# Five score groups in each column by Strassen's seven products, summed two at a time, with all score slots in one tile

## The chip, the cores and the metric

The kernel runs on one core of one Trainium2 chip. The metric is the device time of one execution in microseconds (us); a kernel's time is the median over its runs. A profile is one execution recorded by the hardware profiler. In it PE is TensorE's matmul, PEld its weight load, DVE is VectorE, ACT is ScalarE, POOL is GpSimd and SP is SyncE; L482 is line 482 of the kernel file.

## The reference

A gated attention without softmax is followed by a feed-forward layer with a gate of its own:

```python
batch, seq, d_model = (8, 3008, 256); d_qk = 64
scale = 1.0 / S
scores = scale * np.matmul(z, z.transpose(0, 2, 1))
attn = np.maximum(scores, 0.0) ** 2
out = np.matmul(attn, v)
x = (u * out).astype(np.float32)          # reshaped to 24064 tokens of 256
...
h = x @ w_in                              # 256 -> 2048
g = h * np.cos(h)
return (g @ w_out).astype(np.float32)     # 2048 -> 256
```

All inputs and the output are float32 in device memory; the kernel works on them as 16-bit floats and accumulates in 32 bits. Since the scores are z times its own transpose, the score matrix of a batch is symmetric.

## The kernel before

**Units.** A batch of 3008 tokens is cut into 6 *columns* of 512 queries (the last has 448). Keys are cut into 24 blocks of 128 (the last has 64), four blocks make a *group* R of 512 keys. So a batch has 6 x 6 squares (column c, group R) of 512 by 512 scores. Time is planned by hand in units, 8 to a column, 48 to a batch: `at(t, rank, f)` notes an event, the events are sorted by time and rank, and run in that order. TensorE's matmuls are chained, so they stay in this order; the other engines' instructions are put in order by the scheduler of the language, within their data dependencies and the ordering edges that `after(...)` adds. The edge from `before[-1]` keeps an instruction behind the last matmul emitted so far.

**Scores.** `s_visit` handles three half squares at once: `s_matmuls` (L271) writes six score banks with 64-row matmuls (the two 64-row halves of the array run side by side), then `s_squares` lets ScalarE do the relu (L307) and VectorE the square (L309), into one of 18 slots in SBUF. There are 14 visits in a batch. Only squares with R >= c are computed; the mirrored one comes from a transpose by DMA on SP's queue (`turn_s`, L321). A diagonal square (R = c) is computed as a triangle, four strips of 512, 384, 256 and 128 columns (L288, L293), and its missing parts are filled by three small transposes (L296). Scores run ahead of their use by `lead`, 1.75 columns.

**Attention times v.** For each column the products with v add up in two accumulator banks. The plain path (`av_bank`, L362) takes two matmuls of 512 columns for each block of keys, eight for a group. The other path is Strassen's scheme in Winograd's form: a group is treated as a 2 x 2 matrix of halves (2 x 128 keys by 256 queries) times a 2 x 2 matrix of halves of v (2 x 128 keys by 128 features); `product(b, c, n)` for n = 1 to 7 (L482) does one of the seven products for all groups of the set `WSET[c]`, two matmuls of 256 columns for each group. It needs sums of score halves, made on VectorE in place in the slots: `a_sums1` makes two sums (L439, L441), the second one into an extra slot, and `a_sums2` (L451) makes two more in one operation after products 2 and 5 have read the old contents. `v_sums` makes four sums of v for each group (L409, L411, L412). `keep` (L496 to L507) copies and adds the parts that several results share. `PLAN` says in which unit of the column each product runs (P1 to P7) and where the blocks left over go (A and B, the two accumulators); `SUM1`, `SUM2`, `WADD`, `RADD` and `TSUM` place the sums. `WSET` has groups 0 to 2 in columns 0 to 3, and 0 to 3 in columns 4 and 5. Columns 0 to 3 of the first batch use no such products; of these, columns 0 to 2 are computed directly, without symmetry. The last 64 keys are a 64-row pair of matmuls (`av_half`, L339), and `finish` (L389) multiplies by u.

**Feed-forward.** 47 tiles of 512 tokens. `h_quantum` does 128 of the 2048 hidden features: two matmuls of 512 columns (L516), a sine on ScalarE (L520), a multiply on VectorE (L523). `y_quantum` does four output matmuls of 256 columns (L533) on the tile before; the sixteenth is followed by a copy on ScalarE and a store (L540). Hidden and output quanta are spread evenly through the units.

**Buffers.** PSUM has six work banks (`ps_w`), shared by scores, hidden tiles and output tiles, and two accumulator banks. v lives in a ring of four tiles of eight blocks, three to a batch; all loads (L121) go through POOL's queue, and `hold` keeps a load behind the last matmul emitted so far. Transposes of u, z and scores are issued on SP.

Of the kernel before, what the change touches and what calls it, by code (L numbers as in the profile page):

```python
# [14 lines left out]
def kernel(  # L15
# [33 lines left out]
    NW = 4  # L49
    PLAN = {  # L50
        0: [(1.0, 'P1 P2'), (1.4, 'P5'), (2.35, 'P6 B1'), (2.55, 'B1'), (3.0, 'P7 B1'),
            (3.4, 'P3'), (4.55, 'A1'), (4.75, 'A1'), (5.4, 'P4 B2'), (6.15, 'A1 B2'),
            (6.35, 'A1 B1'), (6.55, 'A2'), (6.75, 'A1'), (7.0, 'A1 B2'), (7.4, 'A3 B1')],
        1: [(1.0, 'P1 P5 P2'), (2.35, 'P6'), (3.0, 'P7 B1'), (3.4, 'P3'), (4.15, 'B1'),
            (4.35, 'A1 B2'), (4.55, 'A1'), (4.75, 'P4 B1'), (5.4, 'B2'), (6.35, 'A1 B1'),
            (6.55, 'A2 B2'), (6.75, 'A5'), (7.0, 'A1'), (7.4, 'B1')],
        2: [(0.75, 'P1 P5 P2'), (1.4, 'P6'), (2.15, 'B1'), (2.75, 'B1'),
            (3.0, 'P7 P3 B1'), (4.55, 'B1'), (4.75, 'B1'), (5.0, 'P4 B1'),
            (5.4, 'A2 B1'), (6.15, 'A1'), (6.35, 'A2'), (6.55, 'A1 B1'), (6.75, 'B1'),
            (7.0, 'A1 B1'), (7.4, 'A4 B1')],  # L60
        3: [(1.0, 'P1 P5 P2'), (2.15, 'P6 B1'), (2.75, 'B3'), (3.0, 'P7'), (3.4, 'P3'),
            (4.55, 'A1 B1'), (5.0, 'A1'), (5.4, 'A1 B2'), (6.15, 'P4 A1'),
            (6.35, 'A1 B1'), (6.55, 'A1 B1'), (6.75, 'A1'), (7.0, 'A2 B1'),
            (7.4, 'A2 B1')],
        4: [(0.75, 'P1 P5'), (1.0, 'P2'), (2.15, 'P6'), (3.0, 'P7'), (3.4, 'P3 A1'),
            (4.35, 'B1'), (4.55, 'P4'), (4.75, 'A1 B1'), (5.0, 'B1'), (5.4, 'B1'),
            (6.15, 'A1 B1'), (6.55, 'A1'), (6.75, 'A1 B1'), (7.0, 'B1'), (7.4, 'A2')],
        5: [(1.0, 'P1 P5'), (1.4, 'P2'), (2.15, 'P6'), (2.55, 'B1'), (3.0, 'P3'),
            (3.4, 'P7 B2'), (4.75, 'A1'), (5.0, 'P4'), (5.4, 'A1 B1'), (6.15, 'A1 B1'),
            (6.35, 'A2'), (6.75, 'A1'), (7.0, 'B2'), (7.4, 'A1')],  # L70
# [181 lines left out]
    def slot(*key):  # L252
        return slots[slot_of[key]].rearrange("p (s k w) -> p s k w", s=K, w=P)

    def seven(b, c):

        return [] if (b, c) <= (0, NC // 2) else WSET[c]

    def s_matmuls(b, c, R, p):


        zt = zT[b % 2]
# [496 lines left out]
```

## Time and profile before

| what | value |
|---|---|
| median of 10 runs | 1214.7 us (1213.78 to 1217.81) |
| the profiled execution | 1214.06 us, its span 1211.9 us |
| granted TensorE clock | 1.00 |
| hidden matmuls L516 / output matmuls L533 | 1504 x 379 ns / 3008 x 273 ns |
| plain products with v L362 / Strassen products L482 | 1024 / 2072 matmuls |
| multiplies L523, squares L309 on VectorE | 752 x 688 ns, 254 x 689 ns |
| sines L520, relus L307 on ScalarE | 752 x 621 ns, 489 x 616 ns |
| from one batch to the next | 150.6 us (column 4's first products start at 385.25 and 535.87) |

How to read it: a mean duration of a matmul contains the time to run through the array, so matmuls that follow each other overlap; what one costs in a stream is the distance from start to start. The same holds, less strongly, for the vector and scalar engines. The chain that ended last is followed back from the last instruction, at each step to what released it. Between two batches of the steady middle part nothing changes but the data, so one batch can stand for six.

### The profile page before, as it was taken

Reading aid. Unit: us, or ns where it says so; the run is one execution under the profiler, and the core shown is the slowest. Engines: PE = TensorE matmul, PEld = TensorE weight load, DVE = VectorE, ACT = ScalarE, POOL = GpSimd, SP = SyncE. Lnnn points to the kernel's source line nnn. Section 1 sums busy time; section 2 is a strip of 40 time slices with the busy share of each in tenths; the row PEclk is TensorE's granted clock in tenths of the full one; section 3 lists DMA queues with packets and bytes.
Section 4 is the critical chain, followed back from the end, with each engine's and each line's share of the span. In section 5 each row is a group of like instructions: output and inputs, shape, how many; then the busy total and the mean of one; then the engine's idle time right before and its main releaser. Section 6 shows DMA issues by size and latency. Waiting matters only on the chain.

```text
span 1211.9 us, 22944 instructions
## 1 busy us (share of the span) xinstructions
PE 1204.7 (99%) x8421; PEld 766.3 (63%) x8421; DVE 1020.5 (84%) x1995; ACT 831.7 (69%) x1741; POOL 146.1 (12%) x201
## 2 busy tenths in 40 slices
PE   8999999999999999999999999999999999999998
PEld 3356666666666666666666666666666666666666
DVE  7888888888888888888888888888888888888875
ACT  6767767677776776767777677676776767767555
POOL 3210101001010010101101101011110111100000
PEclk9999999999999999999999999999999999999999
DMA  9997968679586795957968569596695857956411
GB/s 153 199 161 120 150 98 129 106 120 154 103 119 109 118 155 103 132 103 111 155 103 134 100 112 163 94 133 104 110 162 94 133 105 113 158 94 120 73 33 48
DMA packets 484225, 145.02 MB, mean 120 GB/s; under 512 B 432400, under 2 KB 484112, under 8 KB 484112
## 3 DMA queue, kind: packets, MB, share of 16 engines
q1 hardware_dynamic: 356448, 88.73, 44.4%
q0 software_dynamic: 100400, 29.77, 25.1%
q10 hardware_dynamic: 27264, 25.06, 6.4%
q8 instruction: 66, 1.08, 0.4%
q14 instruction: 47, 0.39, 0.1%
HBM read 60.29 MB, written 24.64 MB: 70 GB/s over the span
## 4 chain that ended last, share of the span: by engine, by line
PE 99%; ACT 1%; DVE 0%; issue 0%; ACTq 0%; DVEq 0%
PE w L533 27%; PE w L516 27%; PE acc L482 19%; PE acc L362 18%; PE w L271 6%; PE acc L339 1%; ACT rt L307 0%; PE w L716 0%; DVE s L309 0%; ACT zT L227 0%; PE w L222 0%; DVE rt L305 0%; DVE x L389 0%; ACT c L520 0%; ACT ob L540 0%
## 5 line engine op out<-in xcount | busy, mean ns | idle before, releaser
L520 ACT ACTIVATE c<-w 128x512 f16<-128x512 f32 x752 | 437.4, 621 | 258.8 <-PE w L516 215.2
L523 DVE TENSOR_TENSOR g<-w,c 128x512 f16<-128x512 f32 x752 | 494.1, 688 | 61.2 <-ACT c L520 59.6
L533 PE MATMUL w<-w_out,g 128*128 128x256 f16 x3008 | 448.6, 273 | 0.0
L516 PE MATMUL w<-x,w_in 128*128 128x512 f16 x1504 | 445.7, 379 | 0.0
L533 PEld LDWEIGHTS <-g 128*128 128x128 f16 x3008 | 294.3, 98 | 191.2 <-issue 0.4
L362 PE MATMUL acc<-s,v 128*128 128x512 f16 (+1 forms) x1024 | 290.6, 378 | 0.4 <-DVE s L309 0.3
L307 ACT ACTIVATE rt<-w 128x512 f16<-128x512 f32 x489 | 253.3, 616 | 44.1 <-PE w L271 44.1
L309 DVE TENSOR_TENSOR s<-rt 128x1024 f16<-128x1024 f16 x254 | 173.0, 689 | 86.0 <-ACT rt L307 84.8
L516 PEld LDWEIGHTS <-w_in 128*128 128x128 f16 x1504 | 147.0, 98 | 73.3 <-issue 3.5
L482 PE MATMUL acc<-s,vsum 128*128 128x256 f16 (+1 forms) x1184 | 154.7, 270 | 0.0
L121 POOL DMA_DIRECT2D ust<-in_u_dram x112 | 81.3, 732 | 556.4 <-PE acc L362 534.8
L362 PEld LDWEIGHTS <-v 128*128 128x128 f16 x1024 | 95.2, 98 | 78.4 <-issue 29.9
L482 PEld LDWEIGHTS <-vsum 128*128 128x128 f16 x1184 | 114.9, 98 | 18.1 <-issue 3.0
L482 PE MATMUL acc<-s,v 128*128 128x256 f16 (+1 forms) x888 | 115.2, 270 | 0.0
L451 DVE TENSOR_TENSOR s<-s,s 128x1024 f16<-128x1024 f16 (+1 forms) x148 | 93.1, 673 | 3.5 <-PE acc L482 3.5
L482 PEld LDWEIGHTS <-v 128*128 128x128 f16 x888 | 83.7, 98 | 19.2 <-issue 11.5
L271 PE MATMUL w<-zT 64*128 64x512 f16 (+3 forms) x684 | 90.4, 359 | 2.4 <-ACT zT L227 1.6
L540 ACT ACTIVATE ob<-w 128x256 f32<-128x256 f32 x188 | 71.3, 379 | 8.4 <-PE w L533 8.4
L288 ACT ACTIVATE rt<-w 128x512 f16<-128x512 f32 (+3 forms) x176 | 62.9, 452 | 11.8 <-PE w L271 11.8
L121 POOL DMA_DIRECT2D v<-in_v_dram x40 | 31.4, 793 | 299.1 <-PE acc L482 146.5
L389 DVE TENSOR_TENSOR x<-acc,ut 128x512 f16<-128x512 f32 (+7 forms) x112 | 64.4, 600 | 2.2 <-PE acc L362 2.1
L441 DVE TENSOR_TENSOR s<-s 128x512 f16<-128x512 f16 (+1 forms) x148 | 60.6, 415 | 1.9
(37 smaller groups left out, 361.3 us busy)
## 6 DMA issues: line engine op xcount, KB each, us to landing
out_dram<-ob ACTq DMA_DIRECT2D x92, 256.0 KB, 2.4
ust<-in_u_dram POOLq DMA_DIRECT2D x80, 128.0 KB, 4.2
v<-in_v_dram POOLq DMA_DIRECT2D x16, 512.0 KB, 6.4
s<-s SPq DMA_TRANSPOSE x249, 4.4
v<-in_v_dram POOLq DMA_DIRECT2D x8, 448.0 KB, 9.5
zst<-in_z_dram POOLq DMA_DIRECT2D x14, 128.0 KB, 4.6
ust<-in_u_dram POOLq DMA_DIRECT2D x16, 96.0 KB, 4.9
w_in<-in_moe_w_in_dram POOLq DMA_DIRECT2D x4, 256.0 KB, 6.4
```

Source lines behind the costliest of these rows:

```text
L121: hold(nc.gpsimd.dma_start(dst, src))
L271: chain(nc.tensor.matmul(sp[:, s0 * P:], zt[h, R * K + k + 1 - lo, :], zt[h, j0 + s0:j0 + K, :].rearrange("p j w -> p (j w)"), start=True, ...
L307: nc.scalar.activation(rt[:, i, :], banks[k], AF.Relu)
L309: ins = nc.vector.tensor_tensor(t.rearrange("p s k w -> p k s w")[:, 2 * p:2 * p + 2], rv, rv, ALU.mult).ins
L362: chain(nc.tensor.matmul(acc[:, 0:wn], vs(b, j // G)[:, j % G, nh * P:(nh + 1) * P], a, start=(start and n == 0), stop=(last and n == len( ...
L451: after(nc.vector.tensor_tensor(dst, src, sub, ALU.subtract).ins, before[-1], NOSYNC)
L482: chain(nc.tensor.matmul(acc[bank][:, cols], lhs[:, k, :], rhs[:, k, :] if old else rhs[:, :, k * P:(k + 1) * P], start=(n in (1, 5) and i ...
L516: chain(nc.tensor.matmul(hp, w_in16[:, k, ft * P:(ft + 1) * P], x[:, k, :], start=(k == 0), stop=(k == NDH - 1)))
L520: nc.scalar.activation(c16, hp, AF.Sin, bias=math.pi / 2.0, scale=inv_s2)
L523: nc.vector.tensor_tensor(gs[(m, ft // FG)][:, ft % FG, :], hp, c16, ALU.mult)
L533: chain(nc.tensor.matmul(ys[m][:, 0:D], gs[(m, f4)][:, ft % FG, ts * P:(ts + 1) * P], w_out16[:, ft, :], start=(ft == 0), stop=(ft == NFT ...
L540: nc.scalar.activation(obs[m][:, i, :], ys[m][:, 0:D], AF.Copy, bias=0.0, scale=inv_s2)
```

## The change

`WSET` gets groups 0 to 4 in every column: 30 groups in a batch in place of 20. All score slots become one tile, so that one access pattern can reach two slots: `teams` pairs neighbouring groups that are stored the same way, and `a_sums1` does its two sums for a pair at once, unless the slots are more than 15 apart. `v_sums` does two groups at once, in four operations; the ordering edge is on the first of them. The second sum has a tile of its own. Diagonal squares become one item of a visit (`t_matmuls`), with their two shorter strips in banks that two diagonals may share. In each visit the third half square is squared on ScalarE (`on_act`). Visits are packed anew, run 2.0 columns ahead, and are shifted singly (`VSHIFT`). The plan tables are all new; the three v loads of a batch move (`VAT`; third before second); hidden tiles come four in a row, followed by sixteen output matmuls (`HOFF`, `YOFF`).

```diff
-    NW = 4
+    NW = 5
     PLAN = {
...
+        3: [(0.75, 'P1 P2'), (1.0, 'P5'), (2.15, 'P6'), (2.35, 'B1'), (2.75, 'P7 P3'),
+            (3.4, 'B1'), (4.75, 'A1'), (5.0, 'A1'), (5.4, 'B1'), (6.15, 'P4'),
+            (6.75, 'A1')],
...
+        5: [(0.75, 'P1 P2'), (1.4, 'P5'), (2.35, 'P6'), (3.0, 'P3'), (4.55, 'P7 B1'),
+            (5.0, 'P4'), (5.4, 'B1'), (6.15, 'A1'), (6.55, 'A1'), (6.75, 'A1'),
+            (7.4, 'B1')],
     }
...
-    TSUM = [-2.9, -0.9, -0.8, 3.5, 3.5]
-    XEND = 4.0
-    WSET = {0: [0, 1, 2], 1: [0, 1, 2], 2: [0, 1, 2], 3: [0, 1, 2], 4: [0, 1, 2, 3], 5: [0, 1, 2, 3]}
+    TSUM = [-1.4, 0.5, 0.1]
+    WSET = {0: [0, 1, 2, 3, 4], 1: [0, 1, 2, 3, 4], 2: [0, 1, 2, 3, 4], 3: [0, 1, 2, 3, 4], 4: [0, 1, 2, 3, 4], 5: [0, 1, 2, 3, 4]}
+    VAT = [-13, -3.9, -4.5]
+    HOFF, YOFF = [0.3, 0.4, 0.4, 0.6], [0.6, 0.7, 0.7, 0.7]
...
-    slots = [kpool.tile([P, K * CW], FP16, name=f"s{i}") for i in range(NSLOT)]
-    vsum = [kpool.tile([P, 4, 2, P], FP16, name=f"vsum{R}") for R in range(NW)]
+    slots = kpool.tile([P, NSLOT, K * CW], FP16, name="s")
+    second = kpool.tile([P, NW, 2, CW // 2], FP16, name="s2")
+    vsum = kpool.tile([P, NW, 4, 2, P], FP16, name="vsum")
...
+    def t_matmuls(b, c, banks, mixed, i):
+        score(b, c, c, 0, 0, 0, banks[0])
+        score(b, c, c, 1, 1, 1, banks[1][:, 0:3 * P])
+        score(b, c, c, 2, 1, 2, mixed[0][:, i * 2 * P:(i + 1) * 2 * P])
+        score(b, c, c, 3, 0, 3, mixed[1][:, i * P:(i + 1) * P])
...
+        if on_act:
+            nc.scalar.activation(sq, rv, AF.Square)
+        else:
+            ins = nc.vector.tensor_tensor(sq, rv, rv, ALU.mult).ins
...
+                s_squares(*pair, banks, on_act=i in (2,) and not direct(*pair[:3]))
...
+    def v_sums(b, g):
+        n = min(2, NW - 2 * g)
+        t = vs(b, g)[:, 0:n * K, :].rearrange("p (r k) (d w) -> p r k d w", r=n, w=P)
+        o = vsum[:, 2 * g:2 * g + n]
+        for d in range(2):
+            ins = nc.vector.tensor_tensor(
+                o[:, :, 2 * d], t[:, :, 2 * d:2 * d + 2, 1], t[:, :, 0:2, d], ALU.subtract).ins
+            if d == 0:
+                after(ins, before[-1], NOSYNC)
+        nc.vector.tensor_tensor(o[:, :, 1], t[:, :, 2:4, 1], o[:, :, 0], ALU.subtract)
+        nc.vector.tensor_tensor(o[:, :, 3], t[:, :, 2:4, 0], o[:, :, 1], ALU.subtract)
...
+    def quarters(b, c, team, first, *step):
+        i, ks, ts = where(b, c, team[0])
+        at = lambda kk, tk: kk * ks + tk * ts
         dims = [(at(*step[0]), 2)] if step else []
+        if len(team) == 2:
+            dims.append(((where(b, c, team[1])[0] - i) * K * CW, 2))
+        return bass.AP(slots.tensor, slots.offset + i * K * CW + at(*first),
+                       (slots.ap[0], *dims, (CW, 2), (1, wide(b, c) // 2)))
...
+    def teams(b, c):
+        out = []
+        for R in seven(b, c):
+            if out and len(out[-1]) == 1 and by_key(b, c, R) == by_key(b, c, out[-1][0]):
+                out[-1].append(R)
+            else:
+                out.append([R])
+        return out
+
+    def a_sums1(b, c, team):
+        if len(team) == 2 and abs(where(b, c, team[0])[0] - where(b, c, team[1])[0]) > 15:
+            for R in team:
+                a_sums1(b, c, [R])
+            return
+        s1 = quarters(b, c, team, (0, 1))
+        after(nc.vector.tensor_tensor(s1, s1, quarters(b, c, team, (1, 1)), ALU.add).ins,
               before[-1], NOSYNC)
         nc.vector.tensor_tensor(
+            s2(b, c, team[0], len(team)), s1, quarters(b, c, team, (0, 0)), ALU.subtract)
...
-    lead = 1.75 * U
-    NV = 3
+    lead = 2.0 * U
+    VSHIFT = {4: -0.27, 13: 0.82, 1: 0.27, 5: 0.0, 2: 0.27, 12: 1.09, 10: 0.27, 7: 0.0, 0: 0.27, 6: 0.29, 9: -0.55, 3: -0.28, 11: 0.54, 8: 0.0}
...
-            at(th + ft // 4 * 2 + ft % 4 * 0.2, 1, lambda m=m, ft=ft: h_quantum(m, ft))
+            at(th + ft // 4 * 2 + HOFF[ft % 4], 1, lambda m=m, ft=ft: h_quantum(m, ft))
...
-                at(th + U + 2 * ts + 0.1 + 0.2 * f4, 4,
+                at(th + U + 2 * ts + YOFF[f4], 4,
...
-                at(t + (-1.5, -0.4, -0.1)[g] * U, 0, lambda b=b, g=g: load_v(b, g))
+                at(t + VAT[g], 0, lambda b=b, g=g: load_v(b, g))
```

## The prediction

> **What bounds the kernel now.** I read the page's busy table and its chain of waits first, then the stretches of equal length, then the chain in order of time, then the groups with shapes kept apart, and last the DMA issues and one score visit in the timeline.
>
> ```profile
> PE 1204.7 (99%) x8421; PEld 766.3 (63%) x8421; DVE 1020.5 (84%) x1995; ACT 831.7 (69%) x1741; POOL 146.1 (12%) x201
> ...
> PE 99%; ACT 1%; DVE 0%; issue 0%; ACTq 0%; DVEq 0%
> ```
>
> TensorE is busy for 99% of the span and makes 99% of the chain that ends last. Busy shares of PE can flatter, so the stretches matter more (time, then busy time of PE, PEld, DVE, ACT, POOL, granted clock, DMA share):
>
> ```profile
> 0.00:50.00 50.00, 46.48 (x245) 16.82 (x246) 41.11 (x72) 32.74 (x61) 14.46 (x24) 1.00 1.25 167
> 300.00:450.00 150.00, 150.00 (x1067) 97.29 (x1065) 128.01 (x254) 105.10 (x222) 17.27 (x25) 1.00 0.79 120
> ...
> 1180.00:1212.00 32.00, 28.78 (x213) 20.45 (x211) 18.02 (x27) 17.42 (x35) 0.00 (x0) 1.00 0.15 51
> ```
>
> From the second batch on PE has no gap, at a granted clock of 1.00; the 7 us that it misses lie in the first 75 us and at the very end. VectorE has 22 us spare in 150, ScalarE 45. So time goes down exactly as matmul columns go away, as long as nothing else becomes late. What a matmul costs in a stream is its pitch in the chain in order of time (start, length, count):
>
> ```profile
> 59.82 2.59 PE acc L362 x12
> ...
> 385.25 2.62 PE acc L482 x24
> 410.06 1.53 PE acc L482 x16
> ```
>
> A 512-column product of the plain path takes 2.59/12 = 215.8 ns, a 256-column Strassen product 2.62/24 = 109.2 ns, a 224-column one (last column of a batch) 1.53/16 = 95.6 ns.
>
> **The change, part by part.**
>
> *Products.* A group (512 keys by 512 queries) costs 8 plain matmuls or 14 half-wide ones. Columns 0 to 3 go from 3 to 5 groups, 4 and 5 from 4 to 5; batch 0 uses the scheme in columns 4 and 5 alone. That is 7 x 8 + 7 + 7 + 2 = 72 more groups, 8 of them in the last, 448-wide column. Building the kernel confirms it: 1024 plain matmuls become 448, 2072 products become 3080. A wide group saves 8 x 215.8 - 14 x 109.2 = 197.6 ns. A 448-column plain matmul has a mean 26 ns under the 512 one:
>
> ```profile
> L362 PE MATMUL acc<-s,v 128*128 128x512 f16 x960 | 273.2, 380 | 0.4 <-DVE s L309 0.3
> L362 PE MATMUL acc<-s,v 128*128 128x448 f16 x64 | 20.0, 354 | 0.0
> L451 DVE TENSOR_TENSOR s<-s,s 128x1024 f16<-128x1024 f16 x116 | 74.1, 688 | 2.7 <-PE acc L482 2.7
> L439 DVE TENSOR_TENSOR s<-s 128x512 f16<-128x512 f16 x116 | 47.8, 419 | 0.0
> L309 DVE TENSOR_TENSOR s<-rt 128x1024 f16<-128x1024 f16 x254 | 173.0, 689 | 86.0 <-ACT rt L307 84.8
> L227 ACT COPY zT<-w 128x1024 f16<-128x1024 f16 x2 | 2.0, 1016 | 2.6 <-PE w L222 2.6
> ```
>
> so 190 ns, and a narrow group saves 8 x 190 - 14 x 95.6 = 182 ns. The sum is 64 x 0.1976 + 8 x 0.182 = **14.1 us less on PE**. Score matmuls stay at 684, feed-forward matmuls at 4512, visits at 14 a batch, each 64-row pair still stands right behind a visit, and SP gets 3 transposes more than its 249; so nothing else moves in amount.
>
> A rule speaks against this step. The Trainium skill (TensorE: Matmul & The Clock Gate, Back-to-back issue gap) says that in a stream of weight loads and matmuls both set the spacing, with about 81 ns at 128 columns and 131 ns at 512. A straight line gives an estimate of 98 ns at 256; eight plain matmuls would be 1048 ns, fourteen products 1372, and the change would add 23 us and end near 1238. The rows above (215.8 and 109.2, proportional to columns, with a weight load before each) contradict it, so I use the rows.
>
> *Vector work*, from the rows above and their 448-wide, 256-wide and v-sum neighbours, by means. Second sums: 148 become 220, 180 x 0.688 + 40 x 0.620 = 148.6 against 93.1, +55.5. First sums: 296 small ones become 88 small and 176 of double size, 72 x 0.421 + 16 x 0.385 + 144 x 0.688 + 32 x 0.620 = 155.4 against 120.6, +34.8. Sums of v: 36.0 against 30.0. One diagonal group more: +1.3. Against that 59 squares go to ScalarE or vanish: -59 x 0.689 = -40.7. Together +57 us: VectorE at 1077 of some 1198, 90%; its spare time in a batch goes from 22 to about 13 us. The cover is that PE waits for none of this directly, only through buffers; ScalarE gets 57 squares at the nearest row, 1.016 us (58 us), and loses 4: 886 us, 74%. I cost both at nothing. A run of four multiplies takes 2.48 us, so one operation more in a queue is worth (2.48 - 0.69)/3 = 0.60; late once in each batch it would cost 7 x 0.6 = 4.2 us (kept as upper bound; a gain is excluded, PE has no wait to lose).
>
> One more price is on a page only. The Trainium skill (ScalarE: Activation LUTs, What ACT_TABLE_LOAD costs) gives about 2.66 us for a switch between table sets. If the new Square were in another set than the sine, 57 x 2 switches would be an estimate of 303 us. The trace shows a single table load, of 1283 ns, and the changed kernel's instruction list also has a single one, so my sum holds nothing for it.
>
> *Waits for banks.* The feed-forward work is regrouped: four hidden tiles in a row, then 16 output matmuls, where before they alternated. A score visit needs all six work banks, so the vector work queued since the last visit must be through. Now the total of PE's waits at visits is 0.5 us. Counting pitches in the changed order, the last hidden tile lies 2.1 to 5.1 us ahead of each visit (1.2 to 2.5 before), and between two visits vector work is at most 0.8 us more than PE's, where 5.1 us of distance follow. I take zero.
>
> *The fifth group of column 3.* Its scores come only just in time. Before product 5 needs the sum, PE has the visit 0.75, the 64-row pair 0.22, 3 plain matmuls 0.65, hidden 1.73, outputs 1.74, products 1 and 2 2.18, eight matmuls of product 5 0.87: 8.1 us. Against it stand, at the same place before the change:
>
> ```profile
> 656.17 0.82 PE L271 MATMUL w<-zT 64*128 64x512 f16 x6
> 656.60 3.05 ACT L307 ACTIVATE rt<-w 128x512 f16<-128x512 f32 x6 [0.53 <-PE w L271]
> 657.71 0.69 DVE L309 TENSOR_TENSOR s<-rt 128x1024 f16<-128x1024 f16 x1 [1.20 <-ACT rt L307]
> ...
> 658.47 4.93 SPq L321 DMA_TRANSPOSE s<-s  x2
> ```
>
> 2.3 us to the issue of the transpose on SP, 4.3 to 5.6 us to its landing (the DMA issues of this place in three batches), 0.42 for the sum: 7.0 to 8.3. That is 0 to 0.2 us, seven times; I take 0.5 us in all. The transpose view has landings of 7.9 us under load; those would cost 2.6 us a batch. While VectorE waits, the hidden-tile multiplies queue behind it, then PE's hidden tiles.
>
> *Loads of v.* The third v load now goes out ahead of the second (on POOL's queue its three DMAs, the second's one, then those of u), behind product 3 of column 5, which frees the ring buffer. Part of its sum carries no ordering edge any more, and in the built order it stands on VectorE right behind two diagonal squares of the visit in that column. PE has 5.7 us between product 3 and that visit (6 hidden 1.30, product 7 0.96, one plain, 2 hidden 0.43, outputs 1.74, product 4 0.96, switch 0.1), then 1.06 to the first square, 0.65 for two: the load has 7.4 us.
>
> ```profile
> v<-in_v_dram POOLq DMA_DIRECT2D x16, 512.0 KB, 6.4
> ...
> v<-in_v_dram POOLq DMA_DIRECT2D x8, 448.0 KB, 9.5
> ```
>
> The last is this very load, at a place where the DMA share was 1.41 (730 to 740 us); the other two v loads, at quieter places, take 6.4. Everything behind the wait shifts: the squares, four multiplies, the column's end, then the sums of v for groups 2 and 3, which product 5 of the next column reads. From the visit to that reading PE has 11.7 us (visit 0.65, pair 0.22, five plain 1.08, 8 and 8 hidden 3.46, 32 outputs 3.48, products 1 and 2 2.18, four matmuls 0.44, switches 0.2), VectorE 3.6 until the visit's work is through, 2.4 for four multiplies, 4.9 for twelve items: 10.9. The second sums right behind, which product 3 reads, are tighter by my count, 0.5 us, and that I take as the slack. I take a landing midway, 8.0 us: 0.6 late, 0.1 after slack, 7 batches, **0.7 us**. Ends: 0, and with the slowest landing seen, 11.4, 3.5 x 7 = 24.5 us.
>
> *The head.* Three such sums (0.42 + 0.42 + 0.29 = 1.1 us) also move into batch 0's first column, where VectorE runs nearly back to back, and score visits start 2 units earlier. Idle gaps of 0.61 and 0.18 us there absorb most: 0.7 us taken, 0 to 2.
>
> *Sum.* -14.1 + 0 + 0.5 + 0.7 + 0.7 = -12.2 us. The profiled execution took 1214.06 (span 1211.9 and 2.1 around it): 1201.9. It lay 0.6 under the median of ten, 1214.7, so I predict **1202.5 us**.
>
> **The rivals.** *The wait for v eats the gain (slower).* One mechanism: the third v load lands after VectorE reaches its sum. At 9.5 us it costs 7 x 1.6 = 11.2, giving 1213; from 14.1 - 1.2 = 12.9, that is a landing of 9.7 us, the change loses; at 11.4 it ends at 1214.7 - 14.1 + 1.2 + 24.5 = 1226. For it: the median of this load. Against it: the place is new, two plain transposes and the next v load share the engines there, not the diagonal's.
>
> *Part of the gain goes into buffers and transposes:* 0.6 to 1.2 us a batch, 4 to 9 us, 1206 to 1211. For it: spare vector time shrinks by 40%. Against it: hidden tiles stand further from the visits.
>
> *VectorE becomes the bound.* If each of 98 visits in seven batches waited for one 0.60 us operation, +59 us, 1260. Against it: 136 us of vector work in 148.6 us of a batch.
>
> *The single tile orders too much.* If sums of two slots waited for every slot between, 88 team sums losing 1 us twice would add about 176 us. Against it: in the built order these sums wait for transposes of their own, and no wait on other readers appears.
>
> **How the numbers follow.** Forecast (1199.5 to 1206) 0.70; part of the gain 0.14; v wait (1211 to 1226) 0.10, 0.03 of it within the bound below; VectorE 0.04; single tile 0.02. A change of 0.2%, 2.4 us, is about what this kernel's measurement can tell from none. Faster: 0.70 + 0.13 = 0.83; within: 0.01 + 0.03 = 0.04; slower: 0.07 + 0.04 + 0.02 = 0.13. The range runs from no wait at all less a pitch error of 1 us, 1199.5, into the second case, 1211, and holds about 0.83.
>
> **What would show it.** The 256-column products at 109 ns and a batch period of 148.6 us instead of 150.6 (385.25 less 234.63 in the chain in order of time): the PE term. A VectorE wait for the v load, or any wait of PE's product line on VectorE near a batch's start: the v term. A VectorE wait on a transpose before column 3: that term. PE waits at the score line summing to more than a few us: the bank term wrong. A product pitch above 112 ns would make the whole prediction wrong.

## The result, and the profile after

| what | before | after |
|---|---|---|
| median | 1214.71 us (31 runs, 1213.64 to 1217.81) | 1222.36 us (9 runs, 1217.28 to 1227.12) |
| ratio | | 1.0065, 95% interval 1.0053 to 1.0078 |
| profiled execution | 1214.06 us, clock 1.00 | 1213.96 us, clock 1.00 |
| mean granted clock of the timed runs | not listed | 0.995 to 1.000, lowest in the longest runs |

The changed kernel is slower by 0.65%, where 12 us of gain were forecast. The profiled execution is not a typical one: it took 1213.96 us, less than any of the nine timed runs. So there are two things to explain. Even at its best the kernel gains nothing; and all nine timed runs take another 3 to 13 us, eight of them with a clock under 1.000. The kernel before has such runs too, but fewer: in all comparisons together 12 of its 129 runs lie above 1217 us, the longest at 1221.38 with a clock of 0.997, against 18 of the changed kernel's 20.

In the changed kernel L260 are the score matmuls of a visit, L316 their relus, L322 and L320 the squares on VectorE and ScalarE, L300 those of diagonals; L529 the Strassen products, L387 the plain ones, L364 the 64-row pairs; L485 and L487 the first sums, L497 the second, L435 to L440 the sums of v, L543 to L554 the copies and additions of `keep`; L563 the hidden tiles, L567 their sines, L570 their multiplies, L580 the output matmuls; L302 and L333 the transposes of diagonal and of whole squares. Its page has the busy time of the engines and the shares of the chain of waits:

```profile
PE 1200.2 (99%) x8853; PEld 808.2 (67%) x8853; DVE 1058.2 (87%) x1980; ACT 861.7 (71%) x1782; POOL 145.7 (12%) x201
...
PE 88%; DVE 4%; DMA 4%; ACT 3%; issue 1%; ACTq 0%; DVEq 0%
```

PE is as busy as before by this measure, but its share of the chain has fallen from 99% to 88%: the other 11 points belong to VectorE, transposes and ScalarE. Stretches of equal length of the same execution (time, then busy time of PE, PEld, DVE, ACT, POOL, clock, DMA share):

```profile
0.00:50.00 50.00, 46.89 (x241) 16.85 (x242) 41.51 (x76) 33.56 (x64) 14.38 (x24) 1.00 1.22 175
300.00:450.00 150.00, 149.88 (x1132) 103.30 (x1130) 134.11 (x253) 109.82 (x228) 17.87 (x24) 1.00 0.81 122
```

VectorE's spare time in 150 us is 15.9 us (22.0 before). The 0.12 us that PE misses here understates its waits, because the modelled end of a matmul covers a short wait. Starts of matmuls show more. Added up by line over six batches of the steady part (from the last 224-column product of the first batch to that of the seventh; each matmul counts until the next one starts, so a wait counts with the matmul ahead of it):

```
us in six batches          before    after    difference
products with v            337.72   327.26     -10.5
score visits                54.71    60.94      +6.2
64-row pairs                11.22    12.34      +1.1
hidden tiles               248.70   250.61      +1.9
output matmuls             251.49   251.91      +0.4
sum                        903.84   903.06      -0.8
```

The products save nearly what they should (11.8 us by the prediction); the visits, pairs, hidden and output tiles, whose matmuls are the same in number and size, give it back. The pitches are unchanged. In the timeline of the changed kernel (start, length), 20 matmuls of 256 columns take 436.39 - 434.21 = 2.18 us, 109 ns each:

```profile
434.21 2.35 PE L529 MATMUL acc<-s,v 128*128 128x256 f16 x20
436.39 0.82 PE L529 MATMUL acc<-s,vsum 128*128 128x256 f16 x6
```

Where a visit is too long, the timeline shows why. Two visits are 6.8 us apart here, at the end of a batch (PE's lines first, then ScalarE's, then VectorE's):

```profile
405.45 1.01 PE L260 MATMUL w<-zT 64*128 64x512 f16 x6
...
406.61 1.98 PE L563 MATMUL w<-x,w_in 128*128 128x512 f16 x8
...
412.23 1.14 PE L260 MATMUL w<-zT 64*128 64x512 f16 x6
...
405.87 3.05 ACT L316 ACTIVATE rt<-w 128x512 f16<-128x512 f32 x6 [0.50 <-PE w L260]
...
409.23 1.12 ACT L320 ACTIVATE s<-rt 128x1024 f16<-128x1024 f16 x1
410.17 1.64 ACT L567 ACTIVATE c<-w 128x512 f16<-128x512 f32 x3
...
409.40 0.62 DVE L485 TENSOR_TENSOR s<-s 128x896 f16<-128x896 f16 x1
...
410.53 0.62 DVE L487 TENSOR_TENSOR s<-s 128x896 f16<-128x896 f16 x1
411.06 1.89 DVE L570 TENSOR_TENSOR g<-w,c 128x512 f16<-128x512 f32 x3
```

Four hidden tiles are written right behind the first visit. Their sines queue on ScalarE behind six relus and the new square (L320), their multiplies on VectorE behind two sums, and the last multiply ends at 412.95. The second visit started at 412.23 and its last two banks are not free: it takes 1.07 us in place of 0.75. The table of waits also has late transposes, those of column 3's fifth group among them (waited for: total, times, longest):

```profile
DVE s L485 <- DMA s<-s: 21.8, 16, 2.9
...
PE acc L529 <- DVE s L485: 2.7, 4, 1.3
```

### The profile page after: what moved, and what is told of

The parts are those of the page before. It is cut to its first block, busy times and chain, and to the rows that moved or that the text cites. A ratio compares the mean times of both kernels' runs of the same rounds, so it can differ in the third digit from the quotient of the medians.

```text
span 1212.1 us, 23879 instructions
## 1 busy us (share of the span) xinstructions
PE 1200.2 (99%) x8853; PEld 808.2 (67%) x8853; DVE 1058.2 (87%) x1980; ACT 861.7 (71%) x1782; POOL 145.7 (12%) x201
## 4 chain that ended last, share of the span: by engine, by line
PE 88%; DVE 4%; DMA 4%; ACT 3%; issue 1%; ACTq 0%; DVEq 0%
PE w L563 25%; PE acc L529 25%; PE w L580 24%; PE acc L387 8%; PE w L260 6%; DMA s<-s 3%; ACT rt L316 2%; DVE g L570 2%; PE acc L364 1%; ACT s L320 0%; ACT c L567 0%; DVE x L414 0%; DVE s L485 0%; DVE s L322 0%; DMA g<-in_z_dram 0%
## 5 line engine op out<-in xcount | busy, mean ns | idle before, releaser
L570 DVE TENSOR_TENSOR g<-w,c 128x512 f16<-128x512 f32 x752 | 478.4, 686 | 37.8 <-ACT c L567 35.2
L567 ACT ACTIVATE c<-w 128x512 f16<-128x512 f32 x752 | 415.5, 633 | 133.7 <-DVE g L570 62.1
L563 PE MATMUL w<-x,w_in 128*128 128x512 f16 x1504 | 368.6, 379 | 0.0
L580 PE MATMUL w<-w_out,g 128*128 128x256 f16 x3008 | 358.4, 273 | 0.0
L580 PEld LDWEIGHTS <-g 128*128 128x128 f16 x3008 | 294.2, 98 | 73.8 <-issue 1.3
L316 ACT ACTIVATE rt<-w 128x512 f16<-128x512 f32 x485 | 249.8, 613 | 40.5 <-PE w L260 40.5
L563 PEld LDWEIGHTS <-w_in 128*128 128x128 f16 x1504 | 145.0, 98 | 159.6 <-issue 14.5
L529 PE MATMUL acc<-s,vsum 128*128 128x256 f16 (+1 forms) x1760 | 216.4, 270 | 3.2 <-DVE s L485 2.7
L529 PEld LDWEIGHTS <-vsum 128*128 128x128 f16 x1760 | 169.3, 98 | 39.2 <-issue 16.9
L322 DVE TENSOR_TENSOR s<-rt 128x1024 f16<-128x1024 f16 x195 | 131.7, 689 | 42.0 <-ACT rt L316 40.1
L529 PE MATMUL acc<-s,v 128*128 128x256 f16 (+1 forms) x1320 | 156.5, 270 | 0.0
L529 PEld LDWEIGHTS <-v 128*128 128x128 f16 x1320 | 128.1, 98 | 16.5 <-issue 2.5
L497 DVE TENSOR_TENSOR s<-s,s 128x1024 f16<-128x1024 f16 (+1 forms) x220 | 136.6, 678 | 0.9 <-PE acc L529 0.9
L387 PE MATMUL acc<-s,v 128*128 128x512 f16 x448 | 128.1, 380 | 0.1
L260 PE MATMUL w<-zT 64*128 64x512 f16 (+3 forms) x684 | 96.9, 361 | 3.0 <-ACT zT L223 1.1
L485 DVE TENSOR_TENSOR s<-s 128x1024 f16<-128x1024 f16 (+2 forms) x132 | 77.5, 587 | 21.9 <-DMA s<-s 21.8
L487 DVE TENSOR_TENSOR s<-s 128x1024 f16<-128x1024 f16 (+2 forms) x132 | 77.7, 589 | 1.3
L387 PEld LDWEIGHTS <-v 128*128 128x128 f16 x448 | 40.1, 98 | 52.7 <-issue 26.7
L543 ACT COPY p<-acc 128x256 f32<-128x256 f32 (+1 forms) x88 | 32.6, 373 | 56.1 <-PE acc L529 55.9
```

What stands on the lines that cost most here:

```text
L260: chain(nc.tensor.matmul(out, zt[h, R * K + k + 1 - lo, :], zt[h, j0 + s0:j0 + K, :].rearrange("p j w -> p (j w)"), start=True, stop=True, ...
L316: nc.scalar.activation(rt[:, i, :], banks[i], AF.Relu)
L322: ins = nc.vector.tensor_tensor(sq, rv, rv, ALU.mult).ins
L387: chain(nc.tensor.matmul(acc[:, 0:wn], vs(b, j // G)[:, j % G, nh * P:(nh + 1) * P], a, start=(start and n == 0), stop=(last and n == len( ...
L487: nc.vector.tensor_tensor(s2(b, c, team[0], len(team)), s1, quarters(b, c, team, (0, 0)), ALU.subtract)
L497: after(nc.vector.tensor_tensor(dst, src, sub, ALU.subtract).ins, before[-1], NOSYNC)
```

## The experiments

In this table the trace of one profiled execution is split at the last 224-column product of the first and of the seventh batch; the rest is the last batch up to the start of the last matmul, behind which another 3.4 to 4.4 us pass in the span. "Wait" is the longest distance between two matmuls at 45 to 95 us. The interval is that of the ratio to the kernel before, measured beside it. The runs s1 to s3, t1_nosums and u1_nosums_v leave out work of the layer; their times serve the argument alone.

| run | median, ratio interval | profiled | first batch | wait | six batches | rest |
|---|---|---|---|---|---|---|
| before | 1214.71 | 1214.06 | 122.5 | 0.6 | 903.8 | 182.2 |
| after | 1222.36, 1.0053 to 1.0078 | 1213.96 | 124.4 | 0.6 | 903.1 | 180.3 |
| e1_again | 1220.42, 1.0029 to 1.0061 | 1216.52 | 128.4 | 3.1 | 900.9 | 181.1 |
| e2_col3 | 1222.58, 1.0018 to 1.0067 | 1229.32 | 138.8 | 6.7 | 903.9 | 180.4 |
| e3_v11 | 1218.22, 1.0013 to 1.0034 | 1218.40 | 128.7 | 2.0 | 904.7 | 179.1 |
| e4_even | 1237.81, 1.0155 to 1.0218 | 1233.95 | 127.8 | 2.9 | 917.5 | 182.3 |
| g1_full33 | 1218.78, 1.0021 to 1.0045 | 1219.79 | 129.3 | 3.2 | 903.9 | 180.7 |
| g2_noact | 1232.46, 1.0113 to 1.0187 | 1231.46 | 130.2 | 3.2 | 915.7 | 180.1 |
| g3_full33_v11 | 1218.26, 1.0016 to 1.0040 | 1217.24 | 127.0 | 1.4 | 905.5 | 179.1 |
| g4_before_tri | 1220.73, 1.0032 to 1.0065 | 1221.75 | 129.9 | 4.5 | 903.8 | 182.2 |
| s1_nosum2 | 1219.94, 1.0027 to 1.0056 | 1220.97 | 132.9 | 7.6 | 901.6 | 180.3 |
| s2_actsmall | 1220.49, 1.0034 to 1.0073 | 1218.66 | 130.1 | 4.2 | 902.8 | 180.3 |
| s3_both | 1218.50, 1.0007 to 1.0053 | 1218.06 | 130.5 | 4.1 | 901.4 | 180.6 |
| s4_head | 1216.12, 1.0001 to 1.0034 | 1215.25 | 125.6 | 2.0 | 903.7 | 180.2 |
| t1_nosums | one run | 1239.45 | 131.9 | 7.5 | 919.6 | 182.4 |
| t2_spread | 1238.23, 1.0178 to 1.0212 | 1240.00 | 134.3 | 6.9 | 917.7 | 181.6 |
| t3_head_spread | 1230.68, 1.0122 to 1.0164 | 1229.53 | 125.0 | 0.6 | 916.8 | 181.8 |
| u1_nosums_v | one run | 1211.94 | 132.0 | 7.7 | 895.8 | 178.7 |
| u2_head_wout | 1215.56, 1.0003 to 1.0033 | 1214.85 | 124.5 | 0.6 | 904.4 | 180.3 |
| u3_head_sums | 1221.01, 1.0037 to 1.0063 | 1222.64 | 127.7 | 1.1 | 907.8 | 181.4 |

The changed kernel's own profile is thus 1.9 us longer in the first batch, 0.8 shorter in six batches, 1.9 shorter in the rest, and 1.0 longer behind the last matmul (4.4 against 3.4), which makes the 0.2 us by which its span is longer.

### First guesses

Three theories stood for the loss: late transposes for column 3 stop VectorE, and TensorE behind it; banks come free late because vector work is late; or the added work draws the clock down ("power"). The changed kernel once more:

> The changed kernel itself, as the yardstick of this set. Its profiled execution took 1213.96 us at a granted clock of 1.00, its nine timed runs 1217 to 1227 us at 0.995 to 1.000. Late-transpose theory: the same spread again, with the time rising as the granted clock falls. Power theory (more vector, scalar and weight-load work draws the clock down): the same too. If neither holds and the extra was chance, most runs lie at 1214 us with a clock of 1.000.

The spread came again (1216.52 to 1224.73). This time the profile caught the extra time, and not where the theories looked: the first batch is 4.0 us longer than in the profile above. Column 3 of that batch in the timeline: PE, the last squares of its diagonal on VectorE, then SP's queue of transposes:

```profile
62.96 0.59 PE L387 MATMUL acc<-s,v 128*128 128x512 f16 x2
66.30 0.38 PE L387 MATMUL acc<-s,v 128*128 128x512 f16 x1 [2.75 <-DMA s<-s]
67.27 3.12 PE L387 MATMUL acc<-s,v 128*128 128x512 f16 x8 [0.59 <-DMA s<-s]
...
47.50 0.42 DVE L300 TENSOR_TENSOR s<-rt 128x256 f16<-128x256 f16 x2
...
36.45 22.45 SPq L333 DMA_TRANSPOSE s<-s  x6
58.99 3.77 SPq L302 DMA_TRANSPOSE s<-s  x3
```

Six transposes of whole squares hold SP's queue from 36.45 to 58.9 us, 3.7 us each, at a DMA share of 1.38 (45 to 60 us). The three small ones of the diagonal square of column 3 (L302) come behind them: their squares were through on VectorE at 47.9 us, they are issued from 58.99 us on, and PE waits for them.

Column 3 back to four groups, in all batches:

```diff
-    WSET = {..., 3: [0, 1, 2, 3, 4], ...
+    WSET = {..., 3: [0, 1, 2, 3], ...
```

> Column 3 goes back to four groups; the fifth is done by plain matmuls, 7 x 0.2 = 1.4 us more on TensorE. Late-transpose theory (VectorE stands still for the transpose of the fifth group of column 3, and TensorE behind it): the two largest waits before the sum vanish, 1208 to 1212 us, clock 1.000 in nearly all runs. Bank theory (TensorE waits at score visits because vector work is late): 1.4 us more than the changed kernel, about 1222 to 1224, waits at the score line unchanged. Power theory: within 2 us of the changed kernel, clock still under 1.000.

Its median is the changed kernel's. The waits of L529 on the first sums go from 2.7 us to 0.2, so that wait was nearly all the fifth group's. VectorE still waits for transposes 11 times, 14.3 us, in place of 16 times, 21.8 us; those are of other squares. But six batches take 903.9 us, no less: the products save 1.2 us, with a dearer plain group and a new 2.2 us wait of L387 on VectorE, and the visits take 63.0 us in place of 60.9. The profiled execution had two waits in the first batch, 6.7 and 5.3 us. So the late transposes of column 3 are not the cause of the loss.

The visit of column 3 and group 4 earlier:

```diff
-    VSHIFT = {..., 11: 0.54, ...
+    VSHIFT = {..., 11: 0.0, ...
-    HALF = {..., 2: 6.2, ...
+    HALF = {..., 2: 4.5, ...
```

> The score visit that makes the second half of the square of column 3 and group 4 stands two units, some 6 us, earlier, and the 64-row pair of column 2 goes with it. Late-transpose theory: the transpose is there long before its sum, 1206 to 1211 us, clock 1.000. Bank theory: as the changed kernel, 1220 to 1225. Power theory: as the changed kernel, clock under 1.000.

The same: the wait on the sum goes to 0.2 us, six batches take 904.7.

Even spread of the feed-forward work:

```diff
-    HOFF, YOFF = [0.3, 0.4, 0.4, 0.6], [0.6, 0.7, 0.7, 0.7]
+    HOFF, YOFF = [0.0, 0.2, 0.4, 0.6], [0.1, 0.3, 0.5, 0.7]
```

> Hidden tiles and output matmuls go back to their even spread through the units. Bank theory, if the regrouping is what makes the visits wait: waits at the score line (now 5.9 us over the usual pitch) go to about zero, 1214 us or less. If the regrouping is what keeps them small: more waits, 1230 us or more. Late-transpose theory: within 3 us of the changed kernel. Power theory: within 2 us of it, clock under 1.000.

14 us more in six batches; visits alone take 71.2 us in place of 60.9, waiting for VectorE's multiplies. With the new placing of products and sums, the regrouping keeps the waits small.

### The first batch

One part of the change put into the kernel before:

```diff
-        return R == c and (b, c) > (0, NC // 2)
+        return R == c and (b, c) >= (0, NC // 2)
...
-            if d or not W:
+            if d:
                 order = [(c + i) % NC for i in range(NC)]
+            elif not W:
+                order = [*range(c + 1, NC), c, *range(c)]
```

> The kernel before the change, with one part of it alone: the square of column 3 and group 3 of the first batch as a triangle with three small transposes, used after groups 4 and 5 and not first. First-batch theory: waits of the plain products L362 on transposes at 60 to 80 us appear, the clock falls under 1.000 in some runs, 1216 to 1224 us. If the transposes alone are not enough (the earlier visits and slots are needed too): 1214 to 1216, clock 1.000. Power theory: unchanged, 1214.7, clock 1.000.

This decides it for the first batch. Three small transposes, once in the program, with the later use of their square, cost the kernel before 6.5 us (1214.18 to 1220.73 on this chip, where none of its 15 runs is above 1216.27), and its six batches stay at 903.84. PE's wait in this run, and the stretches of 2 us around it (columns as above; the clock stands third from the end):

```profile
PE acc L362 <- DMA s<-s: 4.1, 1, 4.1
...
64.00:66.00 2.00, 1.15 (x6) 0.39 (x5) 2.00 (x5) 1.52 (x4) 0.00 (x0) 1.00 2.09 161
66.00:68.00 2.00, 0.00 (x0) 0.00 (x0) 1.45 (x5) 0.00 (x0) 0.00 (x0) 1.00 1.93 151
68.00:70.00 2.00, 0.67 (x2) 0.19 (x2) 0.00 (x0) 0.00 (x0) 0.00 (x0) 0.60 1.72 161
70.00:72.00 2.00, 2.00 (x5) 0.46 (x4) 0.00 (x0) 0.00 (x0) 0.00 (x0) 0.50 1.31 184
72.00:74.00 2.00, 2.00 (x10) 0.63 (x10) 0.59 (x2) 1.22 (x4) 0.00 (x0) 0.50 1.28 273
74.00:76.00 2.00, 2.00 (x9) 0.91 (x8) 1.97 (x7) 1.27 (x5) 0.00 (x0) 0.69 0.88 183
```

PE stands still from 65 to 69.2 us; then it runs at half the clock until about 75 us. Half of some 6 us is 3 us more on top of the 4.5 us gap: 7.4 us in the first batch.

The same part taken out of the changed kernel:

```diff
+            if b == 0:
+                some = [pr for q in some for pr in (
+                    [(0, 3, 3, 0), (0, 3, 3, 1)] if q == (0, 3, 3, 2) else [q])]
```

> Only in the first batch, the square of column 3 and group 3 is computed in full again, as before the change, in place of a triangle with three small transposes. First-batch theory (the added transposes come into a queue that is already late while the DMA engines are full, TensorE waits for them in column 3 of the first batch and the clock drops after the wait): the waits of the plain products L387 on transposes at 60 to 80 us vanish, all runs have a clock of 1.000 and lie at 1212 to 1215 us, as the profile of the changed kernel that had no such wait. Power theory: as the changed kernel, 1217 to 1227 us, clock under 1.000. Steady-state theory (the whole loss lies in the batches after the first): the same as power, 1220.

The wait on transposes is gone, but PE now waits 2.9 us for the last quarter of the second weight matrix, which the regrouped output matmuls would read at 70.1 us (70.9 before):

```profile
PE w L580 <- DMA w_out<-in_moe_w_out_dram: 2.9, 1, 2.9
```

It is the next thing late, at a DMA share of 1.52 (60 to 80 us). Together with the earlier visit:

> The full square of column 3 in the first batch, and the earlier visit for column 3 and group 4 in all. First-batch theory and late-transpose theory together: no wait of L387 on transposes, no wait of the product line for the sum in column 3 (2.7 us in the changed kernel), 1210 to 1213 us at a clock of 1.000. If the earlier visit itself makes banks late: 1214 to 1217.

1218.26 against 1218.78, nothing gained by the visit, as in the steady part of its first trial.

More of the first batch as before: the edit of g1_full33, and

```diff
+            if (b, i) == (0, 10):
+                t += 2
...
-                order = [*range(c + 1, NC), c, *range(c)]
+                order = [(c + i) % NC for i in range(NC)]
...
-            at(th + ft // 4 * 2 + HOFF[ft % 4], 1, ...
+            at(th + ft // 4 * 2 + (HOFF[ft % 4] if m else ft % 4 * 0.2), 1, ...
...
-                at(th + U + 2 * ts + YOFF[f4], 4,
+                at(th + U + 2 * ts + (YOFF[f4] if m else 0.1 + 0.2 * f4), 4,
```

> The changed kernel with the first batch's part as before the change: column 3's own square in full and used first, its visit two units later, the first token tile's hidden and output matmuls spread evenly. First-batch theory: no wait on a transpose or on the second weight matrix at 45 to 85 us, clock 1.000 in nearly all runs, 1211 to 1214 us with little spread, 2 to 3 us under the kernel before at best. If the loss is in the steady part's clock: 1217 to 1222, clock under 1.000.

1216.12, a wait of 1.6 us for the weights left in its profile. With the weights loaded two units earlier as well:

```diff
-                at(19 + 2 * q, 0, lambda q=q: load_w_out(q))
+                at(17 + 2 * q, 0, lambda q=q: load_w_out(q))
```

> The first batch's part as before the change and the second weight matrix loaded two units earlier, the rest as changed. First-batch theory: no wait on a transpose or a weight at 45 to 85 us, clock 1.000 in nearly all runs, the first batch within 2.5 us of the kernel before, 1211 to 1214 us. If the loss of the timed runs has another source: 1217 to 1222, clock under 1.000.

1215.56 us, 12 runs from 1213.72 to 1221.58: some 5 to 7 us under the changed kernel (by the ratios to the kernel before, 1.0018 against 1.0045 and 1.0065), and within 0.33% of the kernel before. The stretch at 60 to 80 us, in the repeated changed kernel and in this one:

```profile
60.00:80.00 20.00, 16.67 (x85) 7.89 (x84) 12.37 (x29) 9.96 (x21) 3.52 (x7) 0.91 1.29 174
```

```profile
60.00:80.00 20.00, 20.00 (x118) 10.49 (x117) 17.55 (x38) 13.58 (x27) 3.85 (x7) 1.00 1.36 175
```

The forecast of the first-batch theory is missed by a little: three of the twelve runs still lie near 1221 us, and there is no profile of one of them.

### The steady batches

All squares back on VectorE:

```diff
-                s_squares(*pair, banks, on_act=i in (2,) and not direct(*pair[:3]))
+                s_squares(*pair, banks, on_act=i in () and not direct(*pair[:3]))
```

> All squares go back to VectorE (57 x 0.69 = 39 us more there, 57 x 1.1 = 63 us less on ScalarE). Theory that the square on ScalarE makes the sines behind it late and so keeps banks from the next visit: waits at the score line fall from 5.9 us to about 2, 1216 us with the first batch as it is. Theory that VectorE has no room: more waits at visits and on sums, 1230 us or more. First-batch theory says nothing of this; the spread with the clock stays.

12.6 us more in six batches: VectorE has no room for 39 us. Next, work taken away. First the second sums, then the squares on ScalarE, then both:

```diff
-                    at(t + SUM2[c][0] + SUM2[c][1] * i, 2.5, lambda b=b, c=c, R=R: a_sums2(b, c, R))
```

```diff
-            nc.scalar.activation(sq, rv, AF.Square)
+            nc.scalar.activation(sq[:, :, :, 0:8], rv[:, :, :, 0:8], AF.Square)
```

> Leaves out the second sums of the score groups (220 operations of 0.69 us on VectorE), TensorE's work is the same. Read from one profile by six batches of the steady part (903.8 us before the change, 903.1 and 900.9 in two profiles of the changed kernel, 892 by the matmuls alone). Theory that VectorE's queue keeps the banks from the visits: 892 to 895. Theory that the square on ScalarE ahead of the sines does it: 899 to 903. Theory that the matmuls themselves are dearer than their pitch: 901 to 903. The first batch keeps its waits.

> The squares on ScalarE are cut to 64 of 1024 columns, so a third of the scores outside the diagonal stays unsquared; ScalarE gets some 50 us of work less, VectorE and TensorE the same. Six batches of the steady part: 892 to 896 if these squares, in front of the sines, make the banks late; 900 to 903 if VectorE's queue does, or if the matmuls are dearer.

> Leaves out the second sums and cuts the squares on ScalarE to 64 of 1024 columns. Bank theory, by whichever engine: 892 us for six batches, which is what TensorE's matmuls come to by their pitches; late transposes alone could add some 2. If the matmuls are dearer than their pitch: 900 or more.

901.6, 902.8 and 901.4 us: within 2 us of the changed kernel's two profiles. By the expectations this spoke for dearer matmuls, which the unchanged pitches exclude. With the squares cut, one visit of each batch (at 476.22 us in the changed kernel) takes 1.07 us in place of 1.24; but in the third of these runs the visit at 567.70 still took 1.07 us in place of 0.75, with first sums in front of the last multiplies, which neither cut touches. So the first sums went too:

```diff
-                    at(t + SUM1[c][0] + 2 * SUM1[c][1] * i, 2,
-                       lambda b=b, c=c, team=team: a_sums1(b, c, team))
```

> Leaves out all sums of score halves on VectorE, the first ones too, and cuts the squares on ScalarE to 64 of 1024 columns; TensorE's work is the same. Theory that sums in VectorE's queue hold the banks: six batches of the steady part in 892 to 895 us, no visit longer than before the change. Theory that the pace is set by the six relus of a visit, behind which the sines of four grouped hidden tiles queue on ScalarE, so that a visit close behind another finds its last two banks not free: 898 to 901, the visits that come 6 us after another still 0.3 us longer, whatever the sums.

919.6, worse, for a reason of its own. Its waits, of PE and of VectorE:

```profile
PE w L260 <- DVE g L570: 15.4, 7, 3.3
```

```profile
DVE vsum L435 <- DMA v<-in_v_dram: 46.1, 14, 5.0
```

VectorE, now early, reaches the sums of v before the third load and then the second have landed, twice a batch, and the multiplies queue behind. That is the prediction's first rival, in a kernel that has too little vector work; the question stayed open. With the sums of v left out as well, after the first batch:

```diff
+        if b:
+            return
         t = vs(b, g)[:, 0:n * K, :].rearrange("p (r k) (d w) -> p r k d w", r=n, w=P)
```

> Leaves out all sums of score halves, the sums of v after the first batch, and all but 64 of 1024 columns of the squares on ScalarE, so that VectorE waits for no load of v and has some 36 us a batch less; TensorE's work is the same. Theory that VectorE's extra operations hold the banks: six batches of the steady part in 892 to 895 us. Theory that the pace of relus, sines and multiplies of the regrouped hidden tiles does it even with light engines: 897 to 901, with waits at score visits and hidden tiles left.

895.8 us: six periods of 149.29 us each. So the load on VectorE and ScalarE, with VectorE's waits for transposes and loads, costs the changed kernel 903.1 - 895.8 = 7.3 us in six batches (5.1 by the repeated profile, 900.9). By lines: products 2.4, visits 4.9, pairs 0.5, output matmuls 0.4, hidden tiles -1.0. The visit shown above at 412.23 us, with the product behind it, in this run (its lines are numbered otherwise: L533 are the products, L567 the hidden tiles):

```profile
417.95 0.82 PE L260 MATMUL w<-zT 64*128 64x512 f16 x6
418.70 1.13 PE L533 MATMUL acc<-s,vsum 128*128 128x224 f16 x10
```

It is back at 0.75 us. Ten of a batch's 14 visits are as long in the changed kernel as here. Two are longer in every batch, this one (1.07 to 1.20 us) and the one at 476.22 (1.24 against 1.07); two more in two of the six batches each (0.91 to 1.33 against 0.59). The longest of these, 0.93 and 1.33, come 3 us behind VectorE's waits of 2.3 and 2.9 us for a transpose, at 158.55 and 761.0 us.

Against the kernel before, the products alone now save 12.9 us, and 4.8 us are lost with light engines too: hidden tiles 2.9, visits 1.3, pairs 0.6. PE's waits of this run name a part, once a batch between a visit and a hidden tile; the four hidden tiles behind the visit and pair at 411.16 us show another, too short for that view:

```profile
PE w L567 <- ACT rt L316: 1.8, 7, 0.3
...
412.24 2.06 PE L567 MATMUL w<-x,w_in 128*128 128x512 f16 x8
```

These eight matmuls, two to a bank, take 1.95 us from the first start to the next line's in place of 1.73: the first of each bank starts at 412.24, 412.72, 413.21 and 413.70, some 0.05 us after a relu ends (412.18, 412.67, 413.16, 413.65). The regrouped order puts hidden tiles right behind a visit, and they get their banks at the pace of the relus.

Could the waits be placed away? Two visits two units earlier, so that no three follow each other closely:

```diff
-    VSHIFT = {..., 1: 0.27, ..., 7: 0.0, ...
+    VSHIFT = {..., 1: 0.0, ..., 7: -0.3, ...
```

> Two of the 14 visits of a batch are put two units earlier, so that no three visits follow each other two units apart. Relu-pace theory: the waits at the visits that are 0.3 to 0.6 us too long fall by half or more, six batches 896 to 900 us in place of 901 to 903; first batch as it is, 1213 to 1220 us in all. Theory of sums in VectorE's queue: 901 to 904, no change.

917.7 us, visits 72.8: worse, both theories wrong about it. The trace shows why: the two moved visits now start 5.8 and 6.4 us behind the visit before (12.6 and 10.9 in the changed kernel), and they are the ones that lengthen, to 1.90 and 1.56 us in each of the six batches (0.59 to 1.33 and 0.75 before the move). They have become two more visits that come too close. With the first batch mended beside it:

> The first batch's part as before the change, the second weight matrix loaded two units earlier, and the two visits earlier as in the run beside it: the candidate for beating both kernels. If the first batch is as harmless as before and the visits no longer wait: 1207 to 1211 us, clock 1.000. If only the first: 1212 to 1214. If the earlier weight load makes transposes late in the full DMA queues: 1216 or more with the clock under 1.000.

The first batch is harmless (125.0, clock 1.00), the steady part is as bad. Last, vector operations moved out from ahead of the two longest waits, with the mended first batch:

```diff
-    SUM1, ... = {..., 5: (-1.55, 0.6)}, ... {..., 1: 5.16, ...
+    SUM1, ... = {..., 5: (-3.5, 0.6)}, ... {..., 1: 4.4, ...
```

> As the run beside it, and two groups of vector operations moved out from between the multiplies ahead of the two visits that wait longest: the first sums of column 5 two units earlier, the last addition of column 1 0.8 units earlier. Theory that single vector operations queued between the last multiplies and a visit hold its banks: the visits that take 0.3 to 0.5 us too long go back to normal, 0.6 to 0.9 us a batch, 4 to 6 us less than the run beside it, 1206 to 1210 us. If the pace of relus and sines decides: within 1.5 us of it; if the moved sums now wait for transposes: slower.

Visits fall to 57.7 us, as meant: single operations ahead of the last multiplies do hold the banks. But a new wait of 1.2 us in each batch, of a plain product on an addition (L387 on L548, 8.2 us in all), more than pays it back: 907.8. It counts with the hidden tiles ahead of it, which take 259.0 us in place of 250.6. No version here that does the whole work is faster than the kernel before.

## Why the prediction was wrong

**Products: right.** "14.1 us less on PE" holds. The pitches stayed at 109 and 216 ns, and six batches save 12.9 us where no engine makes them wait, against 11.8 by the prediction (nine wide groups of 197.6 ns and a narrow one of 182 in a batch, six times).

**The step that failed first: "Waits for banks ... I take zero", and "Vector work ... I cost both at nothing".** Six batches gained 0.8 us in place of 11.8: nearly the whole gain went here. The engines' queues cost 7.3 us in six batches (5.1 by the repeated profile; the prediction's upper bound was 4.2 for the run), and 4.8 are lost even with light engines, most of them where hidden tiles stand right behind a visit. The prediction had this as a rival, "part of the gain goes into buffers and transposes", at 4 to 9 us and a chance of 0.14; it took nearly the whole gain. The error was in the counting. I compared vector work with PE's work between visits and found distance enough. But a bank comes free only after a chain through two in-order queues: six relus (3.05 us), the new square (1.12), the sines, the multiplies, and whatever sum was put between. In the changed kernel that takes 7.5 us from the first visit to the last multiply (405.45 to 412.95), and the next visit came after 6.8.

**The second: "SP gets 3 transposes more than its 249; so nothing else moves in amount".** All three lie in the first batch, behind a queue that is some 11 us late (e1_again), and PE needs them. Put into the kernel before, they cost 6.5 us. The head was costed from VectorE's gaps at 0.7 us, up to 2; SP's queue and the DMA share, 1.25 at 0 to 50 us by my own row (1.41 at 45 to 60 us in the changed kernel), were not weighed. Even without a long wait the changed kernel's first batch took 1.9 us more. Nor was the clock: every row of the profile had 1.00, and I took it as given.

**The fifth group of column 3: right mechanism, too small.** PE loses 2.7 us to it and its like (0.5 predicted), 0.2 with the group taken out. Of VectorE's 16 waits for transposes 11 remain then; the prediction had none for other squares. Removing it gained nothing, since other waits were next in line.

**The loads of v: no cost seen.** The 0.7 us that the sum holds for them did not come: the third load lands in 5.9 us at its new place (8.0 taken), and no wait on it appears. It does appear once VectorE is made early, where PE's visits wait 15.4 us for the multiplies behind it.

**VectorE as the bound, single tile.** VectorE was busy 37.7 us more, not 57 (means of an operation contain overlap with the next), and is not the bound on average. No wait on other slots' readers was seen.

**What stays open.** Timed runs have no trace, so that their extra time lies in the first batch is inferred: their clock is low; every profile with a clock under 1.00 has a wait of 2.9 us or more at 45 to 95 us, but u3_head_sums, which has several short ones, and none with 1.00 has one over 2.0; and mending it took most of the extra away. Against it as the whole account: in g1_full33 three runs of 1219.16 to 1221.70 us have a clock of 1.000, and where their time went is not known. The first batch of the best version is still 2 us longer than before. Why the changed kernel's span has 1.0 us more behind the last matmul is not known, and other placings of the steady part were not tried beyond the ones above.

## What to carry to other kernels

Work that leaves the bounding engine is a gain only if every buffer that it writes comes free as early as it now asks for it: follow the release through each in-order queue, operation by operation, at the place where two users are closest, not by sums between them. Look at what a change does once, in the first stage, where queues are full, as closely as at what it does in each round. And compare the profiled execution with the spread of the timed runs: a profile can be the one that had no wait.

## What the runs showed of the hardware

In these runs the granted clock halved behind waits. Told by the distance between the starts of two matmuls: 3.1 and 1.0 us close together brought a mean of 0.91 over 20 us (e1_again), 4.5 us some 6 us at 0.50 (g4_before_tri). Three of 1.6 to 2.0 us within 6 us left it at 1.00 (e3_v11), while 0.8, 0.9 and 0.6 us within 3 us, behind one of 1.1, brought 0.50 at 90 to 92 us (u3_head_sums). It came in the steady part too, behind 2.3 us (g2_noact, half clock from 775.1 us) and 3.5 us (t1_nosums, from 596.8 us). In the clock's own record each stretch at half clock behind a wait is some 3.4 us long (e1_again, 67.8 to 71.2) or 6.8 us (g4_before_tri, 68.4 to 75.2). The Trainium skill (TensorE: Matmul & The Clock Gate, What's actually happening) has the half clock after an idle window of about 3.4 us, free-running, and the full one after a busy window of as much; the half clock agrees, the lengths are one and two such windows, and that shorter gaps can be enough was seen here. So the wait of 4.5 us in g4_before_tri cost 7.4 us.

In the first batch of e1_again six DMA transposes of whole score squares held SP's queue for 3.7 us each, at a DMA share of 1.38 at 45 to 60 us (one at 68.76 us, at a share of 1.10, took 1.9 us), so that the small ones behind them were issued 11 us after their squares were through on VectorE.
